# First step of the transforms on sums and differences of row pairs, in blocks of 24 by 24 for five n2, from the third batch on

## The chip, the cores and the metric

One Trainium2 chip, one core. The metric is the device time of one execution in microseconds (us), median of the runs of a kernel. The kernel before takes 2937.27 us (median of 3 runs, 2937.0 to 2939.01).

## The reference, cut to what matters

```python
# x: [8, 3008, 256]; filt_r, filt_i: [1505, 256]; w_gate, w_val: [256, 1536]; w_out: [1536, 256]; all float32
X = np.fft.rfft(x, axis=1)
y = np.fft.irfft(X * (filt_r + 1j * filt_i), n=3008, axis=1)
t = y.reshape(8 * 3008, 256)
g = t @ w_gate
out = (g * (1 / (1 + np.exp(-g))) * (t @ w_val)) @ w_out
```

## The kernel before

3008 is 47 x 64, so a transform is done in two steps of small products, then the filter, then two steps back. The kernel loops over the batches. A batch has twelve steps of about 30 us; in each, the products of the second half (tokens by weights) of batch b run on TensorE, and between them, at fixed places of a schedule, pieces of the transform of batch b+1. The first step of that transform, here called the step, lies in steps 0 to 3; the middle steps (`pb`, `pc`) lie in 4 to 10. In the profile, `wk`, `wa` and `we` are the banks that take the products with the first weights, `wA`, `wF` and `wG` those with the last weights, `h` is what these multiply. GpSimd does the halves of sums that are written `h<-h` and `D<-f,f`.

The step before, for 47 rows n1 and 64 columns n2 of a batch: sixteen units, each with 94 rows (n1 and a half of n2) and 2 x 256 columns.

```python
def load_x(self, u):
    ...                                        # batch 0 is loaded in another way
    elif u < N_ONE:                            # N_ONE = 16
        self.x[u] = xpool.tile([NR, NV, C], FP32, ..., tag="x")        # 94 x 2 x 256
        rows = x[self.b].rearrange("(r n) c -> r n c", n=32)
        for r in (slice(0, 80), slice(80, NR)):
            self.load(out=self.x[u][r], in_=rows[r, ts(u, NV), :])

def stage1(self, u):
    t1 = t1pool.tile([NK, NV, C], FP32, ..., tag="t1", bufs=2)         # NK = 96
    ps = self.bank(f"pa_{self.b}_{u}")
    pin(nc.tensor.matmul(out=ps[0:NK], lhsT=wf_t, rhs=self.x.pop(u), start=True, stop=True))
    self.load_x(u + 2)
    yield                                      # the rest comes at a later place of the schedule
    pin(nc.scalar.copy(out=t1, in_=ps[0:NK]))
    pin(nc.scalar.dma_start(out=self.d1_rows[:, ts(u, NV), :], in_=t1))
```

The first two loads of a batch's rows are issued in step 9 of the batch before, `following.load_x(0)` and `(1)`. `pin` keeps an instruction at its place in the order of its engine; each engine works in that order.

## Time and profile before

| what | value | where from |
|---|---|---|
| span | 2935.6 us | the page's header |
| TensorE, VectorE, ScalarE, GpSimd busy | 99, 66, 55, 54% | part 1 |
| period of a batch | 358.54 us | two marks of the chain, below |
| one unit of the step on TensorE | 0.862 us | starts of its matmul and of the next work, median of 112 |

The group of the step's matmuls, from part 5 of the page (line, engine, operation, out<-in, partitions x elements, count; then busy us in all, mean ns of one, idle time of the engine before them), and two marks of the chain of work that ended last, in order of time (start, us, work):

```profile
L590 PE MATMUL pa<-x,wf_t 94*96 94x512 f32 x224 | 114.7, 592 | 0.0
```
```profile
455.70 1.34 PE wA L871 x12
...
814.24 1.34 PE wA L871 x12
```

The first says that the seven batches concerned have 112 units (a float32 matmul is two records), the other two give the period. The table of windows (start:end and length in us, then the busy us of each engine with its count of instructions, the granted clock, the busy share of the DMA engines and their GB/s), for the first step of a batch and for one with a middle step:

```profile
core 0: us, PE busy (x) PEld busy (x) DVE busy (x) ACT busy (x) POOL busy (x), PEclk, DMA share, GB/s
814.24:844.00 29.76, 29.76 (x209) 28.74 (x209) 16.83 (x41) 16.70 (x44) 14.14 (x19) 1.00 0.60 195
...
994.00:1024.00 30.00, 30.00 (x210) 29.56 (x209) 20.33 (x46) 15.54 (x43) 16.55 (x21) 1.00 0.70 224
```

TensorE is busy for the whole of each window. VectorE (DVE) has 13 us of 30 free in the steps with the changed work, and less where the middle steps run.

### The profile page before, as it was taken

How to read it: one execution, taken by the hardware profiler on the slowest of the kernel's cores; microseconds unless marked ns; L12 is line 12 of the kernel's file. 1: busy time of each engine (PE TensorE's matmuls, PEld its weight loads, DVE VectorE, ACT ScalarE, POOL GpSimd, SP SyncE). 2: the span in 40 equal slices, each digit the busy share in tenths (PEclk: the TensorE clock that was granted, in tenths of full speed). 3: DMA queues.
4: the chain of work that ended last, by engine and by line, in shares of the span. 5: the costliest groups of instructions: out<-in, count | busy, mean ns of one | idle time of the engine just before them, and what ended most of it. 6: DMA issues, size and time to landing. Idle time of an engine off the chain costs nothing.

```text
span 2935.6 us, 57374 instructions
## 1 busy us (share of the span) xinstructions
PE 2902.9 (99%) x20040; PEld 2806.8 (96%) x20040; DVE 1927.8 (66%) x4380; ACT 1611.1 (55%) x4208; POOL 1586.1 (54%) x1767
## 2 busy tenths in 40 slices
PE   7999999999999999999999999999999999999999
PEld 5889999999999999999999999999999999999999
DVE  6888765576655776557765667656666566766665
ACT  6775455545555555555555554555555555555554
POOL 4876655556444655456554556454564545555453
PEclk9999999999999999999999999999999999999999
DMA  8677865575555755556646566556665565644442
GB/s 228 212 258 250 299 194 179 179 229 181 178 182 185 223 186 165 190 183 205 213 155 194 183 203 211 165 177 204 194 199 174 176 211 191 200 140 154 148 130 89
DMA packets 225661, 558.82 MB, mean 190 GB/s; under 512 B 32666, under 2 KB 110474, under 8 KB 225374
## 3 DMA queue, kind: packets, MB, share of 16 engines
q1 hardware_dynamic: 190286, 485.84, 52.4%
q10 hardware_dynamic: 26160, 45.43, 4.4%
q0 software_dynamic: 8928, 23.89, 2.3%
q8 instruction: 161, 2.64, 0.4%
q14 instruction: 126, 1.03, 0.1%
HBM read 459.97 MB, written 95.05 MB: 189 GB/s over the span
## 4 chain that ended last, share of the span: by engine, by line
PE 94%; DVE 1%; POOL 1%; issue 0%; ACT 0%; DMA 0%; SPq 0%; DVEq 0%; POOLq 0%
PE wa L792 24%; PE wA L871 17%; PE wk L792 16%; PE we L792 12%; PE wG L871 9%; PE wF L871 4%; PE pa L590 3%; PE pd L697 3%; PE pc L663 2%; PE pb L630 2%; PE pd L700 0%; POOL y_t L245 0%; DVE h L839 0%; POOL wt_t L245 0%; DMA o<-o 0%
## 5 line engine op out<-in xcount | busy, mean ns | idle before, releaser
L792 PE MATMUL wa<-y_t,wt_t 128*128 128x188 f32 x4464 | 879.0, 323 | 3.9 <-issue 1.4
L792 PEld LDWEIGHTS wa<-y_t,wt_t 128*128 128x128 f32 x4464 | 730.2, 190 | 29.1 <-issue 17.7
L245 POOL TENSOR_TENSOR h<-h 128x376 f32<-128x376 f32 x190 | 183.2, 986 | 779.1 <-DVE h L839 759.9
L871 PE MATMUL wA<-wo_t,h 128*128 128x128 f32 x4608 | 576.9, 275 | 1.8 <-DVE o L245 1.1
L871 PEld LDWEIGHTS wA<-wo_t,h 128*128 128x128 f32 x4608 | 563.0, 192 | 15.8 <-issue 11.1
L792 PE MATMUL wk<-y,wt_t 128*128 128x188 f32 x2976 | 565.9, 323 | 0.0
L248 POOL TENSOR_TENSOR h<-h 128x376 f32<-128x376 f32 x570 | 554.4, 995 | 0.5
L792 PEld LDWEIGHTS wk<-y,wt_t 128*128 128x128 f32 x2976 | 478.9, 190 | 25.8 <-issue 19.8
L248 DVE TENSOR_TENSOR we<-we,m 128x376 f32<-128x376 f32 x576 | 318.7, 556 | 194.9 <-PE we L792 134.0
L792 PE MATMUL we<-y_t,wt_t 128*128 128x188 f32 x2232 | 431.5, 323 | 1.4 <-ACT we L823 1.4
L792 PEld LDWEIGHTS we<-y_t,wt_t 128*128 128x128 f32 x2232 | 369.4, 190 | 1.8 <-ACT we L823 1.7
L248 POOL TENSOR_TENSOR D<-f,f 128x376 f32<-128x376 f32 x288 | 281.1, 990 | 103.2 <-ACT f L807 102.5
L252 DVE SCALAR_TENSOR_TENSOR y<-wk,c 128x376 f32<-128x376 f32 x480 | 245.1, 543 | 131.2 <-ACT we L823 54.7
L827 ACT COPY m<-wa 128x376 f32<-128x376 f32 x576 | 272.3, 473 | 86.9 <-PE wa L792 85.8
L834 ACT ACTIVATE g<-wa 128x188 f32<-128x188 f32 x576 | 188.2, 327 | 187.5 <-PE wa L792 180.0
L871 PE MATMUL wG<-wo_t,h 128*128 128x128 f32 x2304 | 288.3, 275 | 0.6 <-DVE o L245 0.6
L871 PEld LDWEIGHTS wG<-wo_t,h 128*128 128x128 f32 x2304 | 281.4, 192 | 0.8 <-DVE o L245 0.8
L834 ACT ACTIVATE u<-we 128x188 f32<-128x188 f32 x576 | 189.1, 328 | 167.8 <-DVE we L248 149.5
L807 ACT ACTIVATE f<-wk 128x376 f32<-128x376 f32 x288 | 139.5, 485 | 234.1 <-PE wk L792 227.2
L811 ACT COPY c<-wk 128x376 f32<-128x376 f32 x288 | 136.2, 473 | 226.2 <-PE wk L792 226.2
L814 DVE SCALAR_TENSOR_TENSOR x<-wk,f 128x376 f32<-128x376 f32 x192 | 104.6, 545 | 233.9 <-PE wk L792 227.7
L823 ACT COPY we<-y 128x376 f32<-128x376 f32 x480 | 224.1, 487 | 32.9 <-DVE h L839 14.3
(144 smaller groups left out, 3904.6 us busy)
## 6 DMA issues: line engine op xcount, KB each, us to landing
wt_t<-w_all SPq DMA_DIRECT2D x174, 896.0 KB
wt_t<-w_all SPq DMA_DIRECT2D x174, 768.0 KB
d<-t ACTq DMA_DIRECT2D x112, 192.0 KB
lent<-later_tbl SPq DMA_DIRECT2D x84, 256.0 KB
lent<-in_filt_r_dram SPq DMA_DIRECT2D x336, 64.0 KB
lent<-d SPq DMA_DIRECT2D x84, 256.0 KB
d<-lent ACTq DMA_DIRECT2D x84, 256.0 KB
x<-in_x_dram SPq DMA_DIRECT2D x112, 160.0 KB
```

The lines of the kernel that those rows point to most:

```text
L245: return eng.tensor_tensor(out=dst, in0=a, in1=b, op=ALU.add)
L248: return eng.tensor_tensor(out=dst, in0=a, in1=b, op=ALU.subtract)
L252: return nc.vector.scalar_tensor_tensor(out=dst, in0=a, scalar=-1.0, in1=b, op0=ALU.mult, op1=ALU.subtract)
L590: pin(nc.tensor.matmul(out=ps[0:NK], lhsT=wf_t, rhs=self.x.pop(u), start=True, stop=True))
L792: pin(nc.tensor.matmul(out=ps[:, z], lhsT=self.wt[:, SLOT[p], z], rhs=rhs, start=start and z == 0, stop=True, skip_group_check=True))
L807: pin(act.mul(self.small(f"f{i}", f"f{i}", 1), t[f"k{i}"], -1.0))
L811: pin(act.copy(out=self.small(f"c{i}", f"c{i}", 1), in_=t[f"k{i}"]))
L814: pin(v.scalar_tensor_tensor(out=dst, in0=t[f"k{j}"], scalar=-1.0, in1=t[f"f{i}" if j == 3 else f"D{at}"], op0=ALU.mult, op1=ALU.add))
L823: pin(act.copy(out=self.bank(f"e{at}"), in_=t[f"y{at}"]))
L827: pin(act.copy(out=self.small(f"m{at}", "m", 4), in_=t[f"a{at}"]))
L834: pin(act.activation(out=self.small(op, "g", 3, 1)[:, 0], in_=ps[:, 1], func=AF.Silu))
L871: pin(nc.tensor.matmul(out=self.tiles[at][:, t, :], lhsT=self.hs[i][:, HID[p], t0:t0 + 128], rhs=wo_t[:, JB * q + i, WO[p], :], start=star ...
```

## The change

A real transform of 47 rows needs, for the real parts, only the sums of the rows n1 and 47 - n1, and for the imaginary parts only their differences: 23 pairs and the row n1 = 0. So a 47-row product becomes two products of about half the rows, and with five n2 side by side these fill the array: 5 x 24 = 120 rows. A unit then has two matmuls of 256 columns and covers five n2; thirteen units do for sixteen. The price is two new VectorE instructions per unit and a further, third buffer for rows. It is done from the third batch on (six batches), since the buffers are lent from the preparation of the weights, which ends in the first batch.

```diff
+def pair(self, u):
+    if u < N_PAIRED:                                     # 13
+        a, b = [self.x[u][0:NP * NPAIR, i] for i in range(2)]      # 115 x 256 each
+        pin(sub(nc.vector, differences[u % 2], a, b))
+        pin(add(nc.vector, a, a, b))
+
+def stage1_paired(self, u):
+    t1 = t1pool.tile([NP * NS, 2, C], FP32, ..., tag="t1", bufs=2)
+    ps = self.bank(f"pa_{self.b}_{u}")[0:NP * NS]
+    table, m = paired_t[0], NP * NS                      # m = 120
+    pin(nc.tensor.matmul(out=ps[:, 0], lhsT=table[:, 0:m], rhs=self.x.pop(u)[:, 0], ...))
+    pin(nc.tensor.matmul(out=ps[:, 1], lhsT=table[0:NP * NPAIR, m:2 * m],
+                         rhs=differences[u % 2], ...))
+    self.load_x(u + 3)
+    yield
+    pin(nc.scalar.copy(out=t1, in_=ps))
+    ... # one store of 120 x 512, contiguous
+    yield
+    self.pair(u + 2)
 def load_x(self, u):
+    elif self.b > 1:
+        ... # t: every third one is the lent buffer x_third
+        self.load(out=t[0:pairs, 0], in_=rows[n2:n2 + NP, 1:NPAIR + 1])     # 115 rows
+        self.load(out=t[0:pairs, 1], in_=back)                              # 115 rows, 47 - n1
+        self.load(out=t[pairs:pairs + NP, 0], in_=rows[n2:n2 + NP, 0])      # 5 rows, n1 = 0
 def load_back():                                         # once, at the end of the first batch
+    pin(nc.sync.dma_start(out=paired_t[0][:, 0:2 * NP * NS], in_=paired_dram.ap()))
 # the plan of a batch
-plan[2], plan[3] = one[6:11], one[11:16]
+plan[2], plan[3] = (one[6:10], one[10:13]) if b else (one[6:11], one[11:16])
-if b + 2 < B and (step, op) == (9, "B01"):
-    for u in range(2):
-        following.load_x(u)
+if b + 2 < B and (step, op) in ((10, "Q2"), (10, "B01"), (11, "Q2")):
+    following.load_x(2 if step == 11 else int(op == "B01"))
+if b + 2 < B and step == 11 and op in ("A02", "B02"):
+    following.pair(int(op == "B02"))
```

(Cut: sizes and host tables, the addresses, and the load of `t2`, which comes in two for one.)

More of the change, by code (lines that the diff above doesn't have):

```diff
@@ L72 @@
 N_TWO = NS // NV
+NP = 5
+NPAIR = N1 // 2
+N_PAIRED = -(-N2 // NP)
 WO = {1: 0, 7: 1, 2: 2, 3: 3, 5: 4, 6: 5, 4: 6}
@@ L152, in dft_tables @@
     de = np.stack([d, d.transpose(2, 1, 0)], 2)
+    paired = np.zeros((NP * (NPAIR + 1), 2, NP, NS))
+    for j in range(NP):
+        paired[NPAIR * j:NPAIR * (j + 1), :, j] = w[1:NPAIR + 1]
+        paired[NP * NPAIR + j, 0, j] = 1.0
+    paired = paired.reshape(NP * (NPAIR + 1), -1)
     pairs = np.arange(128).reshape(2, N2).T.ravel()
@@ L157, in dft_tables @@
     return (wf.reshape(NR, NK).astype(f32), wi.reshape(NK, NR).astype(f32),
-            back.astype(f32), np.ascontiguousarray(de).astype(f32),
+            back.astype(f32), paired.astype(f32), np.ascontiguousarray(de).astype(f32),
             np.ascontiguousarray(later).astype(f32))
@@ L174 @@
     nc = tc.nc
-    wf_host, wi_host, back_host, de_host, later_host = dft_tables()
+    wf_host, wi_host, back_host, paired_host, de_host, later_host = dft_tables()
     wf_dram = nc.inline_tensor(wf_host, name="wf_tbl")
     wi_dram = nc.inline_tensor(wi_host, name="wi_tbl")
+    paired_dram = nc.inline_tensor(paired_host, name="paired_tbl")
     back_dram = nc.inline_tensor(back_host, name="back_tbl")
@@ L471 @@
     TICKS = 20
-    back_t = []
+    back_t, paired_t, differences, third = [], [], [], []
     def load_back():
+        for n in range(3):
+            t = rpool.tile([128, 2, 128], U32, name=f"paired_{n}", tag="pw", bufs=3)
+            t = t.bitcast(FP32).rearrange("p b f -> p (b f)")
+            (differences if n else paired_t).append(t[0:NP * (NPAIR + (not n))])
+        t = rpool.tile([128, 2, 128, 2], U32, name="x_third", tag="raw", bufs=2)
+        t = t.bitcast(FP32).rearrange("p b f two -> p (b f two)")
+        third.append(t[0:NP * (NPAIR + 1)].rearrange("p (i c) -> p i c", c=C))
+        pin(nc.sync.dma_start(out=paired_t[0][:, 0:2 * NP * NS], in_=paired_dram.ap()))
         t = rpool.tile([128, 2, 128, 2], U32, name="back", tag="raw", bufs=2)
@@ L528, in load_x @@
                                   in_=rows[r, 8 * u + a:8 * u + a + n, :])
+            elif self.b > 1:
+                if u < N_PAIRED:
+                    t = third[0]
+                    if u % 3 < 2:
+                        t = xpool.tile([NP * (NPAIR + 1), 2, C], FP32, name=f"x_{self.b}_{u}",
+                                       tag="x")
+                    n2, pairs = min(NP * u, N2 - NP), NP * NPAIR
+                    rows = x[self.b].rearrange("(n1 n2) c -> n2 n1 c", n2=N2)
+                    back = bass.AP(tensor=x.tensor,
+                                   offset=x.offset + ((self.b * N1 + N1 - 1) * N2 + n2) * C,
+                                   ap=[[C, NP], [-N2 * C, NPAIR], [1, C]])
+                    self.load(out=t[0:pairs, 0], in_=rows[n2:n2 + NP, 1:NPAIR + 1])
+                    self.load(out=t[0:pairs, 1], in_=back)
+                    self.load(out=t[pairs:pairs + NP, 0], in_=rows[n2:n2 + NP, 0])
+                    self.x[u] = t
             elif u < N_ONE:
@@ L547, in load_two @@
                 self.t2[u] = lend("t2", u)
-                self.load(out=self.t2[u], in_=self.twos(self.d1, u))
+                if self.b < 2:
+                    self.load(out=self.t2[u], in_=self.twos(self.d1, u))
+                    return
+                rows = self.d1.rearrange("a n c -> (a n) c").rearrange(
+                    "(n s p) c -> p n s c", n=N2, p=2)
+                for i in range(2):
+                    self.load(out=self.t2[u][N2 * i:N2 * (i + 1)], in_=rows[i, :, ts(u, NV)])
         def load_tables(self, i):
@@ L584, in bank @@
             return fbank(name)
+        def pair(self, u):
+            if u < N_PAIRED:
+                a, b = [self.x[u][0:NP * NPAIR, i] for i in range(2)]
+                pin(sub(nc.vector, differences[u % 2], a, b))
+                pin(add(nc.vector, a, a, b))
+        def stage1_paired(self, u):
+            t1 = t1pool.tile([NP * NS, 2, C], FP32, name=f"t1_{self.b}_{u}", tag="t1", bufs=2)
+            ps = self.bank(f"pa_{self.b}_{u}")[0:NP * NS]
+            table = paired_t[0]
+            m = NP * NS
+            pin(nc.tensor.matmul(out=ps[:, 0], lhsT=table[:, 0:m], rhs=self.x.pop(u)[:, 0],
+                                 start=True, stop=True))
+            pin(nc.tensor.matmul(out=ps[:, 1], lhsT=table[0:NP * NPAIR, m:2 * m],
+                                 rhs=differences[u % 2], start=True, stop=True))
+            self.load_x(u + 3)
+            yield
+            pin(nc.scalar.copy(out=t1, in_=ps))
+            n2 = min(NP * u, N2 - NP)
+            rows = self.d1.rearrange("a n c -> (a n) c").rearrange("(r p) c -> r (p c)", p=2)
+            pin(nc.scalar.dma_start(out=rows[NS * n2:NS * (n2 + NP)],
+                                    in_=t1.rearrange("p i c -> p (i c)")))
+            yield
+            self.pair(u + 2)
         def stage1(self, u):
@@ L1075 @@
         d = [three(cur, k) for k in range(1, NCHUNK)]
-        one = [nxt.stage1(u) for u in range(N_ONE)] if nxt else []
+        if b:
+            one = [nxt.stage1_paired(u) for u in range(N_PAIRED)] if nxt else []
+        else:
+            one = [nxt.stage1(u) for u in range(N_ONE)]
         two = []
```

## The prediction

> **What bounds the kernel now.** I read the page of the kernel before in this order: the header and part 1 (who is busy), part 4 (the chain that ended last), part 5 (the costliest groups), then the waits of TensorE and the timeline around one unit of the changed step.
>
> ```profile
> span 2935.6 us, 57374 instructions
> PE 2902.9 (99%) x20040; PEld 2806.8 (96%) x20040; DVE 1927.8 (66%) x4380; ACT 1611.1 (55%) x4208; POOL 1586.1 (54%) x1767
> ...
> PE 94%; DVE 1%; POOL 1%; issue 0%; ACT 0%; DMA 0%; SPq 0%; DVEq 0%; POOLq 0%
> PE wa L792 24%; PE wA L871 17%; PE wk L792 16%; PE we L792 12%; PE wG L871 9%; PE wF L871 4%; PE pa L590 3%; PE pd L697 3%; PE pc L663 2%; PE pb L630 2%; PE pd L700 0%; POOL y_t L245 0%; DVE h L839 0%; POOL wt_t L245 0%; DMA o<-o 0%
> ```
>
> TensorE is busy 99% of the span and carries 94% of the chain; what is not TensorE lies in the start of the first batch and in the tail. The changed step is "pa L590", 3% of the chain. I also asked for the waits of TensorE between 330 and 2560 us: the list was empty. So from the second batch to the seventh TensorE never waits, and the period of a batch (358.5 us from one mark of the chain to the same mark of the next, 455.70 to 814.24 us) is the plain sum of its matmuls. Two things follow. A matmul saved there is saved in full. And any new wait of TensorE is a loss in full, because no idle time is there to take it in.
>
> What one unit of the step costs is read from starts, not from durations, since the profile models the ends of matmuls and they overlap:
>
> ```profile
> 825.26 1.02 PE L590 MATMUL pa<-x,wf_t 94*96 94x512 f32 x2
> 826.12 0.80 PE L792 MATMUL wa<-y_t,wt_t 128*128 128x188 f32 x4
> ```
> ```profile
> 951.83 1.03 PE L630 MATMUL pb<-lent 128*128 128x256 f32 x4
> 952.70 0.80 PE L792 MATMUL wa<-y_t,wt_t 128*128 128x188 f32 x4
> ```
>
> A float32 matmul is two records. One old unit (512 columns, 94 rows) holds TensorE from 825.26 to 826.12; over all 112 units the median from its start to the start of the next work is 0.862 us. The middle step has just the shape that the new unit will have, two matmuls of 256 columns: 951.83 to 952.70, median 0.863 us over 84 cases. Rows and output columns of the array do not show: 94 rows by 96 columns and 128 by 128 run at the same rate per streamed column (0.862/512 = 1.68 ns, 0.863/512 = 1.69 ns).
>
> **What the Trainium skill says.** "FP8 and Floating Point Precision", section TensorE Precision Notes: true FP32 takes four passes through the array. "TensorE: Matmul & The Clock Gate", section Back-to-back issue gap: the spacing follows the streamed columns N, at 2.4 GHz when warm. Together that is 4 x 512 / 2.4 = 853 ns; the trace has 862 and a granted clock of 0.998, so it agrees: only streamed columns count, and fuller rows (120 of 128 for 94) are free.
> "SBUF — State Buffer", section Who interferes with whom: a DVE instruction with two SBUF inputs contends with a GpSimd instruction that reads SBUF, one with at most one SBUF input does not. The new sums and differences have two SBUF inputs; nearly all DVE work of the steady batches has one in PSUM. The first batch has such instructions, and the trace agrees:
>
> ```profile
> 71.96 0.82 DVE L325 TENSOR_SCALAR pw<-wo_t 128x256 uint32<-128x256 uint32 x1
> 72.70 0.95 DVE L245 TENSOR_TENSOR wt_t<-wt_t 128x256 f32<-128x256 f32 x1
> ...
> 76.31 0.75 DVE L245 TENSOR_TENSOR wt_t<-wt_t 128x256 f32<-128x256 f32 x2
> ```
>
> With GpSimd working (71.62 to 74.23 us) a 128x256 sum takes 0.95 us, with GpSimd idle two take 0.75, that is 0.41 each and 0.34 from start to start.
> "DMA: Bandwidth & Descriptors", section Anatomy of one DMA: about 2 us of every transfer are fixed. The smallest time from issue to landing of the x loads of the kernel before is 2.0 us, the median 2.5, the longest 5.4 (behind a block of weights).
>
> **The change, part by part.** Batches three to eight are concerned, 6 of 8, 6 of the 7 whose first step runs beside the products.
> 1. TensorE. Old: 16 units of 512 columns, 16 x 0.862 = 13.79 us per batch. New: 13 units (five n2 each, the last overlapping the one before), each one matmul for the real part with the sums plus the row n1=0 (K 120) and one for the imaginary part with the differences (K 115), both 120 outputs by 256 columns: 13 x 0.863 = 11.22 us. Saved 2.57 us per batch, times 6: 15.4 us. This is the only term on the path that sets the end.
> 2. ScalarE: 13 copies of 120x512 for 16 of 96x512 at 0.58 us: 1.7 us less per batch, beside TensorE, worth nothing.
> 3. VectorE: 26 new 115x256 instructions per batch, 0.34 to 0.95 us each. GpSimd is busy 54%, so about half of them meet it: as an estimate 0.65 each, 1.3 us per unit, 17 us per batch, about 100 us in all; the busy share goes from 66% to about 69%. Beside TensorE if nothing waits for it.
> 4. Loads: per unit two of 115 KB and one of 5 KB in rows of 1 KB (before: 160 and 28 KB in rows of 2 KB); the bytes per batch stay (13 x 240 KB for 16 x 188), the issues go from 32 to 39. The middle step's t2 comes in two loads for one, 12 more issues. At 0.4 us per issue on the SP queue this is 8 us of 358 and hidden. The stores go to 240 KB in one run. DMA engines are busy 50 to 70% and stay there.
> 5. Once: a table load and two buffers lent from the weight preparation, after it has ended; nothing.
> Sum: 2937.27 - 15.4 = 2921.8 us. I add about one microsecond for stray waits and say 2923.
>
> **The rivals.**
> (a) VectorE becomes late and TensorE starts to wait. VectorE works in program order, so a sum of rows that waits for GpSimd or a load holds back the products that TensorE and the banks need. For it: 78 times a block of up to 2 us, in a schedule without spare TensorE time. Against it: the middle steps already put VectorE blocks of 1.4 us (two 692 ns products) and 0.68 us at the same places of the schedule, without one wait of TensorE. I looked at the twelve stretches of a batch: VectorE is busy 16.3 to 17.4 us of 30 in the four stretches of the first step and 19 to 23 in those of the middle steps. With four pairs (5.2 us) the former come to about 22, where the latter run already. If each pair cost TensorE 0.2 us, 78 x 0.2 = 16 us would eat the gain and the time stay at about 2937; at 0.5 us it would be 2960, slower by 0.8%.
> (b) The rows land too late for the sums. A load is issued when the unit three earlier has been multiplied, and the sums want it one slot and a bit later. Adding the measured matmuls between the two places of the schedule gives 8.4 to 9.7 us, more with the transform's own work; against 5.4 us for the longest landing plus 1.2 us for three issues. So there is room, though only two or three microseconds in the worst case. A miss would cost TensorE a few tenths in some units: 2925 to 2935.
> (c) The sums slow GpSimd, whose halves of h the output products wait for. At most 26 x about 0.5 us per batch, against 170 us in which GpSimd idles: nothing.
> (d) The gain was hidden anyway, another engine setting the batch's period. The empty list of TensorE's waits speaks against it.
>
> **Range and chances.** The first term is arithmetic on measured durations, I trust it within half a microsecond per batch. What is uncertain is one-sided: new waits. I give (a) and (b) together a third for a few microseconds and a tenth for eating most of the gain. So 2923, with 8 in 10 between 2919 and 2933. A gain of 2% would need 59 us, and all of the changed step in six batches is only 83; a loss of 2% would need 0.75 us in each of 78 units. Within 2%: 97%; faster 1%; slower 2%.
>
> **What would show it.** Right: the matmuls of this step in later batches are 256 wide and hold TensorE 0.86 us per unit, 13 units; the period of a batch falls from 358.5 to about 356.0; the list of TensorE's waits in the middle batches stays empty or below 5 us; the new VectorE groups have means of 0.5 to 0.8 us; ScalarE's copies of this step fall to about 94. Wrong: rows in TensorE's waits that name VectorE's sums or x, or products and banks that came late right after them; a mean of the new VectorE groups near 1 us or idle time before them that ends with a load; or a unit that takes TensorE visibly more than 0.86 us.

## The result, and the profile after

The changed kernel takes 2925.14 us (median of 4 runs, 2923.87 to 2927.23), beside it the kernel before 2937.14 (4 runs, 2936.94 to 2939.01). The ratio is 0.9958, with a 95% interval from 0.9941 to 0.9976: the same by the 2% mark, and 12 us faster. A ratio here is the mean time of one kernel's fast runs over that of the other's of the same rounds, so not quite the ratio of the medians quoted.

The header and part 1 of the page after:

```profile
span 2922.1 us, 57842 instructions
...
PE 2888.1 (99%) x20160; PEld 2830.6 (97%) x20160; DVE 2030.1 (69%) x4536; ACT 1599.6 (55%) x4190; POOL 1595.3 (55%) x1767
```

TensorE is still what sets the time: 14.8 us less busy, for a span shorter by 13.5. VectorE has 102 us more work and hands none of it on. The step's groups after, and the two marks of the chain:

```profile
L641 PE MATMUL pa<-paired,paired 115*120 115x256 f32 x156 | 46.5, 378 | 0.0
L639 PE MATMUL pa<-x,paired 120*120 120x256 f32 x108 | 32.2, 379 | 0.0
```
```profile
813.35 1.34 PE wA L939 x12
...
1169.38 1.34 PE wA L939 x12
```

The imaginary parts are 156 records, so 78 units, 13 in each of six batches; the second batch keeps its 16 old units (a group of 32 records, left out). The real parts with the lent buffer are the missing 48 of L639. The period is 1169.38 - 813.35 = 356.03 us for 358.54: 2.5 us less per batch, 15.0 in six. Now one new unit, from TensorE's timeline (start, us, line, work):

```profile
824.38 0.60 PE L639 MATMUL pa<-x_third,paired 120*120 120x256 f32 x2
824.81 0.60 PE L641 MATMUL pa<-paired,paired 115*120 115x256 f32 x2
825.25 0.80 PE L860 MATMUL wa<-y_t,wt_t 128*128 128x188 f32 x4
```

From 824.38 to 825.25 are 0.87 us; over all 78 units worked out from the trace it is 0.869 us (0.868 to 0.870).

TensorE's waits, asked for from 330 to 2545 us, are no longer an empty list:

```profile
PE wa L860 <- DVE o L256: 1.4, 1, 1.4
PE pb L698 <- DMA lent<-d: 0.8, 2, 0.5
```

(TensorE's line, what it waited for; us in all, times, longest.) Both lie between 338 and 361 us, in the first batch, and nothing follows up to 2545 us. The first, like others in this kernel, is put down to what came last: in a repeat of the kernel the same wait of 1.3 us stands as `y_t<-yt`, a load, which lands within 0.2 us of it.

VectorE's new groups, from the groups by form (the last number is the idle time before them):

```profile
L256 DVE TENSOR_TENSOR x<-x 115x256 f32<-115x256 f32 x54 | 35.1, 649 | 1.8
L259 DVE TENSOR_TENSOR paired<-x 115x256 f32<-115x256 f32 x54 | 34.2, 633 | 0.0
L256 DVE TENSOR_TENSOR x_third<-x_third 115x256 f32<-115x256 f32 x24 | 28.5, 1189 | 0.8
L259 DVE TENSOR_TENSOR paired<-x_third 115x256 f32<-115x256 f32 x24 | 22.8, 949 | 0.0
```

In all 120.6 us for 156 instructions, 0.77 each. (VectorE's busy time grew by 102 us only, since such records overlap their neighbours: 829.62 + 0.42 is past the next start, 829.96.) The lent buffer seems slower, but it is the place, not the buffer: every third unit's sums come at a place of the schedule right behind the start of GpSimd's halves. VectorE's timeline shows a pair beside an idle GpSimd and one beside a busy one, and GpSimd's shows the latter's neighbours:

```profile
829.16 0.42 DVE L259 TENSOR_TENSOR paired<-x 115x256 f32<-115x256 f32 x1
829.62 0.42 DVE L256 TENSOR_TENSOR x<-x 115x256 f32<-115x256 f32 x1
...
839.77 1.87 DVE L259 TENSOR_TENSOR paired<-x_third 115x256 f32<-115x256 f32 x1
841.67 1.09 DVE L256 TENSOR_TENSOR x_third<-x_third 115x256 f32<-115x256 f32 x1
```
```profile
838.87 1.93 POOL L259 TENSOR_TENSOR h<-h 128x376 f32<-128x376 f32 x2
840.76 0.62 POOL L928 DMA_DIRECT2D out_dram<-o  x1
841.40 1.08 POOL L259 TENSOR_TENSOR D<-f,f 128x376 f32<-128x376 f32 x1
```

The same instruction takes 0.42 us alone, 1.09 where a GpSimd instruction runs, and 1.87 where GpSimd's sum is followed by its issue of a store. All 156, worked out from the trace, give the pattern: 65 meet nothing and take 0.42 us in the median; one meets a GpSimd sum that starts after it, and takes 0.42 too; 84 meet one that they outlast, and end 0.28 us after it has ended; and six, one in each batch, end 0.26 to 0.29 us after the end of such an issue (the one above at 841.64, the issue at 841.37). So it looks as if the issue blocks VectorE's sum as GpSimd's sum does; no run tried an issue by itself. And the first step of a batch in the table of windows, for that shown of before:

```profile
813.35:843.60 30.25, 30.25 (x218) 29.99 (x218) 21.08 (x47) 16.85 (x45) 14.62 (x20) 1.00 0.63 199
```

VectorE went from 16.8 to 21.1 us, and TensorE's column still fills the window. The windows' edges are marks of the work, so a single window's length is not to be compared with that of before; the period is.

The rows land later than before: from issue to landing the median of the 115-row loads, worked out from the trace, is 5.0 us (3.6 to 8.8), of the old 80-row ones from 360 us on 2.5 (2.2 to 8.2). The semaphore of an 80-row load rises in sixteen steps, that of a 115-row load in six: one right behind the issue (for the load issued at 391.08 us it comes at 392.42) and then five engines' (396.99 to 397.85). The Trainium skill explains the number of engines ("DMA: Bandwidth & Descriptors", section Why a DMA increments its semaphore by 16 and not by 1): a transfer is split over the largest number of engines, up to 16, that divides the slowest dimension of both sides. 115 rows out of a source of 5 x 23 leave 5, 80 rows leave 16. The trace agrees. That the fewer engines are what makes these loads late is likely, but not shown: their rows are also shorter (1 KB for 2 KB), and in the same trace loads of 128 rows of 1 KB with sixteen steps (`t<-d`) take 4.35 us in the median. It cost nothing here: VectorE's idle time before the new instructions is 1.8 and 0.8 us in the whole run, and in all 78 units the rows had landed before the difference began, by 1.1 us at the least.

### The profile page after: what moved, and what is told of

Same layout as the page of the kernel before. It is cut to its first block, busy times and chain, and to the rows that moved or that the text cites.

```text
span 2922.1 us, 57842 instructions
## 1 busy us (share of the span) xinstructions
PE 2888.1 (99%) x20160; PEld 2830.6 (97%) x20160; DVE 2030.1 (69%) x4536; ACT 1599.6 (55%) x4190; POOL 1595.3 (55%) x1767
## 4 chain that ended last, share of the span: by engine, by line
PE 93%; DVE 1%; DMA 1%; POOL 1%; ACT 0%; issue 0%; SPq 0%; DVEq 0%; POOLq 0%
PE wa L860 24%; PE wA L939 17%; PE wk L860 16%; PE we L860 12%; PE wG L939 9%; PE wF L939 4%; PE pd L765 3%; PE pc L731 2%; PE pb L698 2%; PE pa L639 1%; PE pa L641 1%; PE pa L658 0%; DMA lent<-later_tbl 0%; PE pd L768 0%; DMA lent<-in_filt_r_dram 0%
## 5 line engine op out<-in xcount | busy, mean ns | idle before, releaser
L256 POOL TENSOR_TENSOR h<-h 128x376 f32<-128x376 f32 x190 | 182.9, 983 | 765.5 <-DVE h L907 755.9
L259 POOL TENSOR_TENSOR h<-h 128x376 f32<-128x376 f32 x570 | 562.4, 1008 | 0.5
```

The costliest lines, as they stand in the source:

```text
L256: return eng.tensor_tensor(out=dst, in0=a, in1=b, op=ALU.add)
L259: return eng.tensor_tensor(out=dst, in0=a, in1=b, op=ALU.subtract)
```

## The experiments

The theories. The traces leave a small question and a larger one. The small one: the steady batches give 15.0 us, the timed runs 12 to 13.4. Theory 1: something is paid once, about 2 us at the end of the first batch, and the new table's load there is the suspect. Its rival: the first 370 us scatter by themselves, in both kernels. The larger one: why did 156 new VectorE instructions cost TensorE nothing? Either there was room to spare, as the prediction argued from the windows, or they just fit.

To see where time goes I compared, in each trace, the start of the same TensorE matmul (the step's own left out) with that in the first trace of the kernel before. A minus is earlier. This "position" is worked out from the traces, and is given at 366 us, where the first batch's last irregular wait is over (its products go on to about 455 us), and at the end.

**e0, the change again.** No edit.

> The changed kernel once more, beside the next three on one chip. Theory 1 (each batch from the third on gains 2.5 us, 6 x 2.5 = 15 us, and the table's load gives a one-off 2 to 2.5 us back at the end of the first batch): 12 to 13 us under the kernel before. Rival (the missing 3 us are only scatter between runs): the gain comes nearer to 15 us, and the trace shows no jump of TensorE between 330 and 365 us.

Measured: 2924.4 us (5 runs, 2923.77 to 2925.69), before 2938.43 (9 runs); ratio 0.9953 [0.9941, 0.9966]. The result repeats. Position +1.24 at 366 us, -13.53 at the end. The wait at 338 us has here another name, which speaks for a load, and not VectorE, as what ended the first line of the list above:

```profile
PE wa L860 <- DMA y_t<-yt: 1.3, 1, 1.3
```

**e1, the table loaded late.** The load leaves the end of the weights' preparation for the last step of the first batch.

```diff
-        pin(nc.sync.dma_start(out=paired_t[0][:, 0:2 * NP * NS], in_=paired_dram.ap()))   # in load_back
+    def load_paired():
+        pin(nc.sync.dma_start(out=paired_t[0][:, 0:2 * NP * NS], in_=paired_dram.ap()))
+    chore(11, "P0", load_paired)
```

> The changed kernel, but the table of sines and cosines is loaded two steps later (start of the last step of the first batch) instead of in front of the weights and middle-step tables. Theory 1: the wait of TensorE of 1.4 us near 338 us shrinks to below 0.9 us and those of 0.8 us for t2 go; 1.5 to 2.5 us less than the changed kernel, so about 2922.5 to 2923.5. Rival (the loss comes from other moves of loads, or is scatter): no difference to the changed kernel, within 0.5 us.

Measured: 2924.08 us (5 runs, 2922.97 to 2928.34), 0.9954 [0.9942, 0.9967]. No difference to e0, so the 1.5 to 2.5 us did not come. The wait at 338 us is shorter, 0.8 us, as Theory 1 foretold, but those for `lent<-d` still sum to 0.8; and the trace has lost 1.7 us between 330 and 366 us as the others have, though the table is loaded only at 423 us. Theory 1 finds no support in the place of the load.

**e2, no sums and differences** (a wrong result). The matmuls take the rows as loaded.

```diff
-                pin(sub(nc.vector, differences[u % 2], a, b))
-                pin(add(nc.vector, a, a, b))
+                pass
...
-                                 rhs=differences[u % 2], start=True, stop=True))
+                                 rhs=rows2, start=True, stop=True))     # self.x[u][0:115, 1]
```

> The changed kernel without the sums and differences on VectorE (wrong result on purpose): the matmuls take the raw rows. Theory 1 (VectorE's 156 new instructions lie wholly beside TensorE): the same time as the changed kernel within 0.7 us, and a batch's period of 356.0 us as before, while VectorE is busy 121 us less. Rival (late sums hold up TensorE somewhat in every batch, 2.51 us gained for 2.57 reckoned, or more in unprofiled runs): 1 us or more under the changed kernel.

Measured: 2925.02 us (5 runs, 2923.11 to 2930.56), 0.9957 [0.9943, 0.997]: the same as with the sums. The period is 356.0 us in both. So the new VectorE work is wholly hidden, not cheap: one batch, whole, in the changed kernel and (second) in e2:

```profile
813.00:1169.00 356.00, 356.00 (x2501) 351.83 (x2500) 246.10 (x551) 191.55 (x502) 190.54 (x204) 1.00 0.59 191
```
```profile
457.00:813.00 356.00, 356.00 (x2502) 351.82 (x2501) 229.09 (x525) 191.56 (x502) 189.24 (x205) 1.00 0.60 191
```

VectorE (third of the busy columns) is 17 us less busy in e2, with 26 instructions fewer; TensorE's column is the same.

**e5, the kernel before with the table's load** (loaded at the same place, not used).

```diff
+        t = rpool.tile([128, 2, 128], U32, name="paired_0", tag="pw", bufs=3)
+        t = t.bitcast(FP32).rearrange("p b f -> p (b f)")[0:NP * (NPAIR + 1)]
+        pin(nc.sync.dma_start(out=t[:, 0:2 * NP * NS], in_=paired_dram.ap()))   # paired_dram: ones
```

> The kernel before with nothing but a load of 115 KB (a table of that size, not used) at the place where the changed kernel has it. Theory 1: slower than the kernel before by 1.5 to 2.5 us, with TensorE waiting near 338 us and for t2 near 348 and 361 us. Rival (the load is harmless): the same as the kernel before within 0.5 us.

Measured: 2938.73 us (5 runs, 2937.62 to 2943.32), 1.0006 [0.9993, 1.0019]. Two of the five runs, at 2942.6 and 2943.3, make its mean; three stand where the kernel before stands. Inconclusive by itself: the interval would still hold the 2 us. The one trace, of the run with 2943.3, does show the waits that Theory 1 asks for (1.8 us at 338 us, 0.4 for `lent<-d`); but e6 below, without the table, waits 1.3 us at 338 us too.

These four ran together.

**e4, one matmul less** (a wrong result). The imaginary part isn't computed; the copy is made of the real part twice.

```diff
-            pin(nc.tensor.matmul(out=ps[:, 1], lhsT=table[0:NP * NPAIR, m:2 * m],
-                                 rhs=differences[u % 2], start=True, stop=True))
...
-            pin(nc.scalar.copy(out=t1, in_=ps))
+            for i in range(2):
+                pin(nc.scalar.copy(out=t1[:, i], in_=ps[:, 0]))
```

> The changed kernel without the second matmul of a unit, that of the differences (wrong result on purpose; ScalarE copies the first one's columns twice). Theory (TensorE's streamed columns set the end, nothing else is near): 78 x 0.434 us = 33.9 us less than the changed kernel, so about 2890.5, and a batch's period of 350.4 us. Rival (another engine or the transfers set a floor just below): less than 28 us less, with waits of TensorE in the middle batches.

Measured: 2893.32 us (4 runs, 2892.09 to 2894.84), 0.9846 [0.9831, 0.9861]. That is 31.8 us under the changed kernel's 2925.14. A unit now holds TensorE for 0.435 us, so 78 x (0.869 - 0.435) = 33.9 us were to be had: most of it came. (Part of the 31.8 is the first batch's scatter: from 366 us on the trace of e4 gains 29.3 us on the first trace of the changed kernel.) A part turned into a wait, from the list of 430 to 2500 us:

```profile
PE wa L859 <- ACT wa L885: 1.6, 5, 0.3
```

The two copies are what was added, and they are ScalarE's; the 0.3 us per batch named here and slower matmuls right behind the wait make about 0.6 us per batch, most of the missing part. The rival's floor (less than 28 us) is not there, but its waits are. The lesson of e4: TensorE's columns are worth their full time, up to the point where another engine's next deadline comes.

**e3, the difference three times** (the result stays right).

```diff
-                pin(sub(nc.vector, differences[u % 2], a, b))
+                for _ in range(3):
+                    pin(sub(nc.vector, differences[u % 2], a, b))
```

> The changed kernel, but each difference of rows is taken three times over (right result), so VectorE has four instructions per unit for two; about 1.3 us more per unit, 100 us in all. Theory (VectorE's sums are beside TensorE with room to spare): the batch's period stays within 0.5 us of 356.0 and the time within 2 us of the changed kernel's 2924 to 2925. Rival (VectorE is at the edge where the steps have four units): TensorE waits appear, 0.3 us or more per unit, 2945 us or more.

Measured: 2985.9 us (4 runs, 2980.34 to 2989.18), 1.0158 [1.0144, 1.0172]: 61 us more than the changed kernel. So there is no room to spare. TensorE's waits from 430 to 2600 us:

```profile
PE wa L861 <- DVE wa L883: 13.6, 6, 2.3
PE wF L940 <- DVE h L908: 9.3, 12, 0.8
...
```

They come six to twelve times, once or twice in each batch, at the same places, and sum to 33.0 us with the three lines left out. A part of the rest is in what follows them. TensorE's timeline at one of these places:

```profile
905.91 1.50 PE L940 MATMUL wG<-wo_t,h 128*128 128x128 f32 x12
908.17 0.90 PE L861 MATMUL wk<-y,wt_t 128*128 128x188 f32 x4 [0.76 <-DVE h L908]
909.84 0.49 PE L940 MATMUL wF<-wo_t,h 128*128 128x128 f32 x2 [0.76 <-DVE h L908]
911.11 2.50 PE L940 MATMUL wF<-wo_t,h 128*128 128x128 f32 x10 [0.78 <-DVE h L908]
```
```profile
910.00:912.00 2.00, 1.22 (x6) 1.03 (x7) 1.51 (x5) 0.70 (x2) 1.16 (x2) 0.69 0.00 0
912.00:914.00 2.00, 2.00 (x10) 1.90 (x10) 0.00 (x0) 0.00 (x0) 2.00 (x3) 0.50 0.00 0
```

Ten records take 2.50 us, where twelve of the same size take 1.50. The windows give the reason in the column before the DMA share: the granted clock is 0.69 and then 0.50. By the trace's own record of it, it falls to a half at 910.74 us, in the third of three waits of 0.8 us within 4 us, and is back at 914.16; the same comes at the same place of each of the six batches. One wait of 2.3 us alone, at 857 us, left it at 1.00. The Trainium skill describes a like case of another kernel ("TensorE: Matmul & The Clock Gate", section A second HAM failure mode: psum-queue depth-cycling): frequent short idle times between groups of matmuls make the clock go to and fro between half and full. The trace agrees, with these numbers. Against the first trace of the changed kernel, that of e3 loses 57 us from 366 us on: 33 are waits, about 10 the low clock (an estimate, six times 3.4 us at half speed), and some 14 I can't account for. Of the forecasts, the rival's held.

**e6, the kernel before again**, one look, for the scatter of its first batch.

> The kernel before once more, for a second trace. Theory 2 (what the prediction and the trace differ by is mostly the first 370 us, whose transfers and waits fall differently in every run, of either kernel): its TensorE work stands 1 to 6 us later than in the first trace of the kernel before already at 370 us and stays at that distance to the end, within 0.2 us. Rival (the first batch of the kernel before is steady and the change costs it 2 us there): it lies within 0.5 us of the first trace everywhere.

Measured: 2940.23 us in one run (its state is unknown, as of any single run). Position +2.06 at 221 us, +2.87 at 344 us, and +2.87 from there to the end. So a kernel identical to the first differs by 2.9 us, all of it in the first 350 us, and by nothing after.

**e7, the change for the last three batches only.**

```diff
-            elif self.b > 1:
+            elif self.b > 4:
...                                     # the plan and the loads likewise
```

> Pairs of rows in the last three batches only, the old step in the others. Theory 2 (a fixed gain of 2.5 us per batch): 3 x 2.5 = 7.5 us under the kernel before, about 2930.5 to 2931.5, and a batch's period of 358.5 us until the fourth boundary and of 356.0 after. Rival (a one-off cost of 2 to 3 us goes with the change): 5 to 5.5 us under the kernel before.

Measured: 2932.34 us (5 runs, 2930.25 to 2933.74), 0.9977 [0.9964, 0.9989]. Position +3.95 at 366 us, then +1.45, -1.03, -3.53 behind the three batches: 2.5 us for each. Up to 366 us this program is the changed kernel's, with the table's load at 335.97 us, so its +3.95 says nothing of the old first batch. The timed runs lie 6.65 us under the kernel before of their call (2938.99), between the theory's 7.5 and the rival's 5 to 5.5, and don't decide.

**e9, the difference twice.** One step between the changed kernel and e3: `for _ in range(2)`.

> The changed kernel with each difference taken twice (right result): one more VectorE instruction per unit. Theory 3 (at the tightest of the 13 places of a batch VectorE is 0.83 us early; the run with two more instructions lost the excess over that): the extra instruction meets GpSimd there and takes 1 to 1.6 us, so TensorE waits 0.2 to 0.8 us once or twice per batch, 2 to 10 us more than the changed kernel, 2926 to 2935. Rival (the loss is proportional to VectorE's work, 61 us for 156 instructions): 30 us more, 2955.

Measured: 2941.59 us (4 runs, 2940.65 to 2942.31), 1.0011 [0.9995, 1.0026]: 16.5 us over the changed kernel, the whole gain is gone. Both forecasts missed, for Theory 3 knew only the first of the two places below. The waits from 430 to 2600 us:

```profile
PE wa L861 <- DVE wa L883: 6.8, 6, 1.1
PE wF L940 <- DVE h L908: 5.9, 12, 0.8
```

Two places per batch. The margin at each can be read in the changed kernel, from VectorE's and TensorE's timelines:

```profile
843.87 0.54 DVE L882 SCALAR_TENSOR_TENSOR wa<-wk,D 128x376 f32<-128x376 f32 x1
...
894.30 0.35 DVE L907 TENSOR_TENSOR h<-we,u 128x188 f32<-128x188 f32 x1
```
```profile
845.24 1.44 PE L860 MATMUL wa<-y_t,wt_t 128*128 128x188 f32 x8
...
894.64 1.50 PE L939 MATMUL wF<-wo_t,h 128*128 128x128 f32 x12
```

At the first place VectorE has freed the bank at 843.87 + 0.54 = 844.41 and TensorE comes for it at 845.24: 0.83 us to spare. At the second, `h` is done at 894.655 (the trace has it to the nanosecond), and the weight load of `wF` that waits for it starts at 894.753: 0.10 us. Where TensorE does wait here, in e9, that load starts 0.05 us after `h` is done, so only 0.05 us of it is spare. In the first trace of the kernel before, the same two hand-overs have 2.07 and 0.92 us (worked out from the trace; without the sums, in e2, 2.07 and 0.91): the new sums use up most of it. A further instruction of up to 1.9 us in front of either is more than is left. The loss per batch is 2.9 us.

**e10, the sums on GpSimd.**

```diff
-                pin(sub(nc.vector, differences[u % 2], a, b))
-                pin(add(nc.vector, a, a, b))
+                pin(sub(nc.gpsimd, differences[u % 2], a, b))
+                pin(add(nc.gpsimd, a, a, b))
```

> The changed kernel with sums and differences on GpSimd in place of VectorE. Theory 3 (what counts is how late the last engine in the chain to TensorE is at one place; GpSimd's differences D follow right behind and feed it): GpSimd takes about 0.82 us each, 1.65 us per unit, D comes 1.65 us later at the tight place, and TensorE waits there: 0.3 to 1.5 us per batch, in all 2 to 10 us more than the changed kernel. Rival (GpSimd idles 45% of the time, so it is the better place): the same time as the changed kernel, within 1 us.

Measured: 2924.51 us (4 runs, 2923.95 to 2925.07), 0.9953 [0.9939, 0.9966]: as good as the changed kernel, not better, and the list of TensorE's waits from 430 to 2600 us is empty. So the rival's forecast held and Theory 3's did not: at the first of the two places 0.75 us are left, at the second 0.92. In the window of the same whole batch as shown with e2, TensorE is again busy for all of 356.00 us, VectorE is back at 228.87 and GpSimd (last busy column) went from 190.54 to 207.23, each new instruction taking 0.73 us. The load moved from one engine to the other, and neither is what the batch waits for. If the new VectorE work had been costing a few microseconds in the changed kernel, they would have come back here; they did not.

**e11, the kernel before with the table in memory** (one more tensor in the chip's memory, neither loaded nor used).

```diff
+    paired_dram = nc.inline_tensor(np.ones((NP * (NPAIR + 1), 2 * NP * NS), np.float32), name="paired_tbl")
```

> The kernel before with the new table only lying in memory, never loaded. Theory 2 (the rest of the difference is scatter of the first 370 us): the same as the kernel before within 0.6 us. Rival (the table shifts where the other tensors lie, and the transfer-bound first batch gets slower by it): 1.5 to 2.5 us slower than the kernel before.

Measured: 2938.2 us (5 runs, 2936.19 to 2939.16), 0.9998 [0.9985, 1.001]; position +0.03 from 344 us to the end. A shift of other tensors in memory is not the cause of anything here.

**What they say of the first 370 us.** Up to 366 us there are two kinds of programs. The changed kernel and its variants, e7 too, carry the new table's load (e1 only later) and the lent buffers, e5 the load and one buffer. They stand at 366 us at +1.60 (the first after), +1.24 (e0), +5.43 (e1), +3.80 (e2), +0.68 (e3), -0.44 (e4), +5.77 (e5), +3.95 (e7), +1.45 (e9) and +1.86 (e10), mean 2.5. The kernel before, e6 and e11 carry neither and stand at 0 (by definition), +2.87 and +0.03, mean 1.0. Between 330 and 366 us alone the former lose 0.2 to 3.2 us, mean 1.7, and the latter 0, 0.8 and 0.5. Every trace of the changed step that adds no work then gains 2.5 us per batch (one batch of e0 2.3, one of e1 1.9). The timed runs, taken together, have 13.4 us between the kernels (means 2938.4 of 31 runs and 2924.9 of 9), 1.6 us less than 15.0; from the scatter of the runs (standard deviations 1.4 and 1.2 us) this is uncertain by about 0.9 us, an estimate. So a cost of 1 to 2 us paid once is likelier than chance, though three traces without it are few. What of the change causes it stays open: the wait at 338 us comes in e6 and e11 too, and moving the table's load (e1) gave nothing.

## Why the prediction was right

Its point was 2923 us, the time is 2925.14, inside the range of 2919 to 2933 and within 2%.

*TensorE, the only term on the path.* Right in kind: e7 shows that the step's matmul time is gained batch by batch and in full, 2.5 us for each of its three; e4 brought 29.3 us of 33.9 behind the first batch's scatter. The term was a little too large. It took the new unit for the shape of the middle step, 0.863 us; it is 0.869. So 16 x 0.862 - 13 x 0.869 = 2.49 us per batch and 15.0 us in six, for the predicted 15.4; the period of 356.03 was foretold as about 356.0. That fewer rows in the array don't matter held. The prediction's 853 ns is an estimate from the two pages that it cites. The second ("TensorE: Matmul & The Clock Gate", section Back-to-back issue gap) gives its spacing by N for a single matmul, and for a stream of weight loads and matmuls a shorter one, 131 ns for N = 512; the 862 ns measured here, 215 for each of four passes, go with the first and not with the second.

*ScalarE.* Foretold 94 copies of the step, found 94 (78 of 120x512 at 585 ns and 16 of the old kind), and nothing on the path.

*VectorE's cost.* Right in kind (0.42 us alone, 1.09 to 1.87 beside GpSimd). The records are longer than estimated, 0.77 us each for 0.65, since more of them meet GpSimd than half (91 of 156), and one in each batch sits through a sum and a DMA issue of GpSimd's. In busy time, where they overlap their neighbours, the forecast of 100 us was met: 102, and 17 per batch by e2. The busy share of 69% was foretold; e2 shows that all of it is hidden. Two of the four groups, with means of 0.95 and 1.19 us, show what the prediction named as a sign of being wrong, and TensorE did not wait for them. (The first line of its fence from 71 us on is no sum but an instruction with one SBUF input. It too is longer beside GpSimd: 0.82 us, where four of its kind that meet nothing take 0.28. So not every one-input instruction is free of GpSimd.)

*Rival (a), VectorE becomes late.* It did not come, but the reason given against it was weak. The prediction argued from sums over a window: 22 us of 30 busy, as in the middle steps, hence room. e9 and e3 show that the sum over a window says little. With one more instruction per unit VectorE is busy 22.4, 23.5 and 25.8 us in the three stretches of 30 to 31 us from 816 us on, so 5.2 us or more are free in each, and yet it costs 16.5 us, with waits in the second stretch as in the third; two more cost 61. What counts is the margin at each place where TensorE waits for VectorE, 0.83 us at one and 0.10 us at another, where the kernel before had 2.07 and 0.92. The change fits into these margins by 0.05 us; I had not measured them, and with some other placing of the pairs it might not have. That this rival stayed away was luck as far as the prediction goes.

*Rival (b), rows too late.* It did not come; VectorE idled 2.6 us in all before the sums. But the reckoning used the landing times of the old loads, up to 5.4 us (two at 369 us, in the same trace, took 7.9 and 8.2), and the new ones take up to 8.8; the three issues of a unit take 2.1 to 3.0 us and not 1.2. With a lead of 8.2 us at the least, and not 8.4, the rows came 1.1 us early at the tightest unit, and not two or three.

*Rival (c), GpSimd slowed.* Its halves went from a mean of 995 to 1008 ns, and nothing came of it, as foretold. *Rival (d), the gain hidden anyway*, falls with the period.

*Stray waits.* About one microsecond was added for them. The list has 2.2 us, both lines in the first batch; as said above, 1 to 2 us paid once there are likely, and their cause is open.

*Two sums.* A loss of 2% would have needed 0.95 us in each of 78 units and not 0.75, for the gain has to be eaten first ((59 + 15) / 78). And a unit's loads are 235 KB, not 240. Neither bears on the forecast.

## What to carry to other kernels

In a kernel whose TensorE never waits, the cost of a matmul is its streamed columns (1.68 to 1.70 ns each here, in float32): fill the array's rows to stream fewer, and count the gain from starts of work, per unit, not from busy shares. Work added on another engine is free only as far as the margin at each hand-over goes, so look for the places where that engine's last result comes just before TensorE needs it; a busy share of 69% told nothing of a margin of 0.10 us. And put differences of a few microseconds down to a cause only after the unchanged kernel has been run again: here its first batch alone moves by 3 us.

## What the Trainium skill lacked or had wrong

- "TensorE: Matmul & The Clock Gate": its summary asks for no idle time over about 3 us between matmuls. In the third of three waits of 0.76 to 0.78 us within 4 us the granted clock fell to a half for 3.4 us (e3), and ten records took 2.50 us for the 1.50 of twelve; one wait of 2.3 us did not bring it down. The section on micro-idles describes the effect, but gives no length or number of idles that sets it off.
- "TensorE: Matmul & The Clock Gate", section Back-to-back issue gap: no figure there tells apart two pairs of matmuls with the same columns. Two of 256 columns with 120 and 115 rows and 120 outputs took 0.869 us, two with 128 and 128 took 0.863, one of 512 columns took 0.862.
- "SBUF — State Buffer", section Who interferes with whom: it calls the shared ports an exclusive lock that blocks the loser until the other's whole instruction is done, and the trace agrees; it doesn't say how soon a blocked sum then ends. Of 91 VectorE sums of 0.42 us that met GpSimd, 84 ended 0.28 us after GpSimd's sum had ended, taking up to 1.49 us. It also holds, as an inference, that such a sum and GpSimd's descriptor work need different interfaces; six sums here ended 0.26 to 0.29 us after GpSimd's issue of a DMA and took 1.87 to 1.90 us, which speaks against it, though no run tried an issue alone.
- "DMA: Bandwidth & Descriptors": the rule of the divisor holds (115 rows as 5 x 23: five engines). What it costs in time at this size isn't given there: a load of 115 KB in rows of 1 KB took 5.0 us to land in the median, where 160 KB in rows of 2 KB on sixteen engines took 2.5; how much of that is the number of engines no run here shows.
